# How a two-column offset gets into a constant table: an addition on VectorE, or two index operations on GpSimd

## The chip, the cores and the metric

One core of a Trainium2 chip. The metric is the time of one execution on the device in microseconds (us). The kernel before takes 411.8 us (median of three runs, 411.5 to 411.99). All runs below were judged to be in the fast state. A verdict of "faster" or "slower" needs a change of over 2%, which is 8.2 us here.

## The reference, cut to what matters

The program is an RWKV-style attention (4 batches, 8 heads, 768 tokens, head dimension 48) followed by a mixture of 8 experts in which each token goes to one expert.

```python
for t in range(S):                               # attention, per batch and head
    cur = einsum('bhd,bhe->bhde', u[None] * kt, vt)
    y[:, :, t] = einsum('bhd,bhde->bhe', rt, state + cur)
    state = w[None, :, :, None] * state + einsum('bhd,bhe->bhde', kt, vt)
...
fresh_e = int(np.argmax(logits[b, s]))           # experts: first maximum wins
e = fresh_e if s == 0 or local_gate[b, s] < 0.5 else prev_e
...
out[b, s] = p[e] * (relu(x[b, s] @ w1[e]) @ w2[e])
```

The kernel has to sort the experts by how many tokens each got. `tie` is a constant table of 8 numbers (the same on all 128 partitions) that makes equal counts distinct and moves the first two experts down by a fixed amount. It matters only that `tie` holds the right eight numbers by the time that the experts are sorted, late in the program.

## The kernel before

Attention runs as 16 items (a batch and a pair of heads). TensorE does the matrix products of an item; GpSimd scales keys and receptances for the item to come (`ke`, `rw`, `pd`); VectorE masks scores (`am`), scans states (`S`) and scales keys (`kw`); loads run some three items ahead. The table is made in passing while item 6 is in work:

```python
def constants(self, part):                       # part 2, in the item loop at n = 5
    ...
    self.tie = self.iota("tie", [P, E], [[-1, E]], base=E - 1, cast=True)
    self.ief = self.iota("ief", [1, E], [[1, E]], cast=True)

def cast(self):                                  # in the item loop at n = 6
    for f, i in self.casts:
        self.nc.scalar.copy(f, i)                # integer -> float, on ScalarE
    self.casts = []
    self.nc.vector.tensor_scalar(self.tie[:, :EARLY], self.tie[:, :EARLY],
                                 float(-E * TAIL), None, Alu.add)

def blocks(self):                                # 88 us later: the only reader of tie
    ...
    nc.vector.scalar_tensor_tensor(self.c8, end, float(E), self.tie, Alu.mult, Alu.add)
```

The place in the loop, cut to the calls around it:

```python
            if n + 1 < M:
                self.scale(n + 1)                # GpSimd: ke, rw, pd of the next item
            ...
            self.inside(n - 1)
            self.before(n - 1)
            if n == 6:
                router.cast()                    # ScalarE casts, then the addition
            ...
            self.scores(n, 0)()                  # TensorE L284, then VectorE am (L286)
            keep = self.scores(n, 1)
            ...
            self.own(n)                          # TensorE L265
            keep()                               # VectorE: second am
```

In the trace VectorE does its work one after another in this order. The `am` product of item 6 is issued just behind the addition, and the next TensorE group (L319, the `turn` of an earlier item) writes the bank that this `am` has to have read. So the addition stands in front of TensorE, by way of `am`.

## Time and profile before

| of the profiled execution | value |
|---|---|
| span | 410.2 us |
| TensorE busy | 393.6 us, 96% |
| VectorE, GpSimd, ScalarE busy | 37%, 35%, 18% |
| mean granted TensorE clock | 0.983 |
| first expert product / last TensorE instruction | 125.5 us / 402.7 us |

The lines that carry the argument are in the prediction below. Two views complete them. From the page: the busy share of the DMA engines (tenths) and what they moved in each fortieth of the span (10.3 us), and the queue that fetches instructions.

```profile
DMA  7999956999224783600641181253245145163010
GB/s 259 414 422 414 414 200 233 320 318 394 82 54 167 291 342 110 266 0 30 231 200 33 54 306 59 59 190 157 67 154 197 53 150 197 41 229 131 0 35 34
...
q8 instruction: 29, 0.48, 0.4%
```

In slices 2 to 5 (10 to 51 us) the DMA engines are full and move 414 to 422 GB/s; then, during the stall, they fall to 200. The queue at the bottom will matter later: instructions come over the same DMA engines, 0.48 MB of them.

The second is a table of stretches (busy us of each engine and, in brackets, instructions; then the granted clock, the DMA share and GB/s).

```profile
core 0: us, PE busy (x) PEld busy (x) DVE busy (x) ACT busy (x) POOL busy (x), PEclk, DMA share, GB/s
46.00:50.00 4.00, 3.60 (x91) 2.56 (x87) 2.16 (x3) 1.31 (x6) 4.00 (x6) 1.00 1.04 410
50.00:54.00 4.00, 0.00 (x0) 0.00 (x0) 4.00 (x1) 0.00 (x0) 4.00 (x5) 0.68 0.83 336
54.00:56.00 2.00, 0.79 (x4) 0.79 (x5) 2.00 (x4) 0.00 (x0) 0.27 (x1) 0.50 0.10 39
56.00:58.00 2.00, 2.00 (x26) 1.67 (x26) 1.75 (x3) 0.70 (x2) 0.00 (x0) 0.50 0.44 104
...
62.00:64.00 2.00, 2.00 (x54) 1.20 (x45) 1.02 (x2) 0.80 (x1) 1.69 (x3) 1.00 0.69 264
```

From 50 to 54 us TensorE ran nothing and VectorE one instruction. The clock was already falling there (mean 0.68), stayed at 0.50 and was back at 1.00 from 62 us. The clock record itself has one low stretch of 10.24 us, which began about 51.4 us.

### The profile page before, as it was taken

The page shows a single profiled execution, that of the slowest core. Times are in us where ns is not written, and L with a number is a line of the kernel's source. Part 1 is how long each engine was busy: PE and PEld are TensorE (multiplying, and loading weights), DVE is VectorE, ACT ScalarE, POOL GpSimd, SP SyncE. Part 2 cuts the span into 40 slices and gives each one's busy share as a digit, 9 for nine tenths or more (in the row PEclk, how much of TensorE's full clock was granted, in tenths as well). Part 3 has the DMA queues.
Part 4 walks back from the last instruction along what each step waited for, and adds up shares of the span by engine and source line. Part 5 has one row for each costly group of instructions (what it writes and reads, how often), then busy time and mean ns, then how long its engine had stood idle before and what let it go on. Part 6 is the DMA issues. An engine that isn't in the chain of part 4 may idle for free. (4 is left out here: it accounts for less than half of the span.)

```text
span 410.2 us, 8245 instructions
## 1 busy us (share of the span) xinstructions
PE 393.6 (96%) x3427; PEld 280.5 (68%) x3427; DVE 149.9 (37%) x322; ACT 72.9 (18%) x175; POOL 143.7 (35%) x178
## 2 busy tenths in 40 slices
PE   8999869999999999999999999999999999999992
PEld 7777656877768999545555555566666666679972
DVE  7887667688953642312211111121121111021201
ACT  4122202222223111111111110111011111111110
POOL 8689948686340043011423102301401301202011
PEclk9999959999999999999999999999999999999998
DMA  7999956999224783600641181253245145163010
GB/s 259 414 422 414 414 200 233 320 318 394 82 54 167 291 342 110 266 0 30 231 200 33 54 306 59 59 190 157 67 154 197 53 150 197 41 229 131 0 35 34
DMA packets 17468, 74.90 MB, mean 183 GB/s; under 512 B 2734, under 2 KB 6591, under 8 KB 14864
## 3 DMA queue, kind: packets, MB, share of 16 engines
q1 hardware_dynamic: 10048, 56.89, 36.8%
q0 software_dynamic: 3424, 9.54, 7.2%
q10 hardware_dynamic: 3952, 7.87, 5.1%
q8 instruction: 29, 0.48, 0.4%
q14 instruction: 15, 0.12, 0.1%
HBM read 64.85 MB, written 9.54 MB: 181 GB/s over the span
## 5 line engine op out<-in xcount | busy, mean ns | idle before, releaser
L1045 PE MATMUL h<-exT,w1t 128*128 128x192 f32 (+7 forms) x480 | 138.8, 428 | 0.0
L1057 PE MATMUL y<-hT,w2t 128*128 128x192 f32 (+7 forms) x432 | 131.3, 440 | 0.0
L1045 PEld LDWEIGHTS h<-exT,w1t 128*128 128x128 f32 x480 | 86.3, 190 | 37.4 <-issue 14.8
L1057 PEld LDWEIGHTS y<-hT,w2t 128*128 128x128 f32 x432 | 77.3, 190 | 31.9 <-issue 13.2
L1104 POOL DMA_INDIRECT out_dram<-yo,sid x27 | 26.8, 992 | 183.5 <-DVE yo L1103 159.7
L1049 ACT ACTIVATE hT<-h 128x192 f32<-128x192 f32 (+7 forms) x72 | 31.9, 444 | 199.6 <-PE h L1045 195.2
L1032 DVE COPY exT<-etp 128x384 f32<-128x384 f32 (+7 forms) x29 | 14.3, 495 | 98.4 <-PE etp L1031 98.4
L1103 DVE TENSOR_SCALAR yo<-otp,gate 128x384 f32<-128x384 f32 (+7 forms) x27 | 16.6, 616 | 91.6 <-PE otp L1101 91.6
L1018 POOL DMA_INDIRECT xg<-x_d,gid x29 | 29.8, 1026 | 45.7 <-DVE sm L867 25.8
L286 DVE TENSOR_TENSOR am<-pair,kept 128x768 f32<-128x768 f32 x32 | 30.1, 952 | 15.5 <-PE pair L284 15.4
L218 POOL TENSOR_TENSOR pd<-rk 128x384 f32<-128x384 f32 x32 | 31.8, 1014 | 3.2 <-DMA rk<-in_rk_dram 2.2
L293 PE MATMUL y<-am,kv 128*64 128x128 f32 x384 | 28.6, 287 | 0.8 <-DVE y L269 0.6
L214 POOL TENSOR_TENSOR ke<-kv,endT 128x288 f32<-128x288 f32 x32 | 24.9, 798 | 8.6 <-issue 3.9
L231 POOL TENSOR_TENSOR rw<-rk,tab 128x384 f32<-128x384 f32 x26 | 23.6, 926 | 8.2 <-PE y L306 8.2
L293 PEld LDWEIGHTS y<-am,kv 128*64 128x64 f32 x384 | 24.8, 142 | 1.6 <-DVE y L269 1.2
L284 PE MATMUL pair<-rw,kw 48*64 48x64 f32 (+1 forms) x768 | 23.0, 249 | 0.5 <-issue 0.3
L284 PEld LDWEIGHTS pair<-rw,kw 48*64 48x64 f32 x768 | 19.9, 134 | 1.9 <-issue 1.0
L310 ACT COPY xT<-y 128x768 f32<-128x768 f32 (+1 forms) x16 | 12.5, 780 | 40.6 <-PE y L306 40.6
L319 PE MATMUL pair<-ident,xT 128*128 128x128 f32 x90 | 13.8, 292 | 5.7 <-DVE am L286 5.6
L319 PEld LDWEIGHTS pair<-ident,xT 128*128 128x128 f32 x90 | 10.1, 146 | 13.3 <-DVE am L286 11.2
L269 DVE TENSOR_TENSOR y<-y,vT 128x768 f32<-128x768 f32 x16 | 15.4, 962 | 3.1 <-PE y L265 3.0
L1031 PEld LDWEIGHTS etp<-ident,xg 128*128 128x128 f32 (+7 forms) x87 | 10.2, 140 | 8.3 <-issue 5.9
(215 smaller groups left out, 284.3 us busy)
## 6 DMA issues: line engine op xcount, KB each, us to landing
w1t<-in_w_dram SPq DMA_DIRECT2D x9, 1536.0 KB, 6.5
w2t<-in_w_dram SPq DMA_DIRECT2D x9, 1536.0 KB, 7.7
rk<-in_rk_dram SPq DMA_DIRECT2D x15, 768.0 KB, 9.8
kv<-in_kv_dram SPq DMA_DIRECT2D x16, 584.0 KB, 9.1
vT<-in_vT_dram SPq DMA_DIRECT2D x16, 384.0 KB, 7.4
x_d<-x ACTq DMA_DIRECT2D x4, 1152.0 KB, 9.6
w1t<-in_w_dram ACTq DMA_DIRECT2D x1, 1536.0 KB, 8.0
w2t<-in_w_dram ACTq DMA_DIRECT2D x1, 1536.0 KB, 11.2
```

The lines of the kernel that those rows point to most:

```text
L214: nc.gpsimd.tensor_mul(t["ke"][:, p::2], t["k"][:, p::2], spread(self.endT[:, p, hp], 1, C2))
L218: nc.gpsimd.tensor_mul(t["pd"][:, z], t["rT"][:, z], t["kT"][:, z])
L231: engine.tensor_mul(t["rw"][:, z], t["rT"][:, z], spread(pw, 1, z.stop - z.start))
L284: nc.tensor.matmul(sc[f * DP:(f + 1) * DP, h, i, x:], lhsT=t["kw"][q, c, o * DP:(o + 1) * DP], rhs=t["rw"][q, c, x:], start=True, stop=True)
L286: return lambda: nc.vector.tensor_mul(t["am"][:, g], sc, spread(self.kept[:, g:g + 3], 1, 2))
L293: nc.tensor.matmul(t["y"][p * DP:(p + 1) * DP, h, c2 * P:(c2 + 1) * P], lhsT=t["v"][:, (2 * c + h) * DH:(2 * c + h) * DH + DP], rhs=t["am" ...
L319: nc.tensor.transpose(banks[h][:, c2 * P:(c2 + 1) * P], xT[:, h0 + h, c2 * P:(c2 + 1) * P], self.ident)
L1018: self.nc.gpsimd.indirect_dma_start(out=xg[:n], out_offset=None, in_=self.x_d[:rows], in_offset=bass.IndirectOffsetOnAxis(ap=u["gid"][:n, ...
L1045: nc.tensor.matmul(h[:, :n], lhsT=u["w1"][:, m, kk, :], rhs=u["xT"][:, kk, :], start=(kk == 0), stop=(kk == DK - 1))
L1049: nc.scalar.activation(u[m], h[:, :n], Act.Relu)
L1057: nc.tensor.matmul(u["y"][d][:, :n], lhsT=u["w2"][:, m, d * P:(d + 1) * P], rhs=u[m], start=(m == 0), stop=(m == FK - 1))
L1104: nc.gpsimd.indirect_dma_start(out=self.outs.pop(), out_offset=bass.IndirectOffsetOnAxis(ap=u["sid"][:n, c:c + 1], axis=0), in_=yo[:n], in ...
```

## The change

Its intent: build the two parts of `tie` with their final values, by two index operations with different bases, so that no addition is needed on VectorE.

```diff
-            self.tie = self.iota("tie", [P, E], [[-1, E]], base=E - 1, cast=True)
+            self.tie = self.tl("tie", [P, E])
+            for x, (z, base) in enumerate(((slice(0, EARLY), E - 1 - E * TAIL), (slice(EARLY, E), E - 1 - EARLY))):
+                i = self.iota(f"tie{x}", [P, z.stop - z.start], [[-1, z.stop - z.start]], base=base)
+                self.casts.append((self.tie[:, z], i))
             self.ief = self.iota("ief", [1, E], [[1, E]], cast=True)
...
         for f, i in self.casts:
             self.nc.scalar.copy(f, i)
         self.casts = []
-        self.nc.vector.tensor_scalar(self.tie[:, :EARLY], self.tie[:, :EARLY], float(-E * TAIL), None, Alu.add)
```

## The prediction

> **What bounds the kernel now.** I read the page's busy shares first. TensorE (PE) is busy for 96% of the span, VectorE (DVE) for 37%, GpSimd (POOL) for 35%, so work taken off VectorE is worth nothing unless TensorE waits for it. The 40 slices then show one hole in TensorE: slices 5 and 6 of the clock row, the only low ones before the last.
>
> ```profile
> PE   8999869999999999999999999999999999999992
> DVE  7887667688953642312211111121121111021201
> POOL 8689948686340043011423102301401301202011
> PEclk9999959999999999999999999999999999999998
> ```
>
> Next, the waits of TensorE. One stands out, and it comes once:
>
> ```profile
> PE pair L319 <- DVE am L286: 5.6, 1, 5.6
> PE pair L149 <- POOL ident masks.py:199: 1.6, 1, 1.6
> PE y L293 <- DVE y L269: 0.6, 2, 0.4
> ```
>
> TensorE stood for 5.6 us until VectorE had done an `am` product. To see why VectorE was late I read its instructions in order of time from 42 to 64 us (columns: start us, us taken, engine, line, operation, tiles; in brackets the idle time before it and what ended it):
>
> ```profile
> 46.54 0.65 DVE L255 TENSOR_TENSOR_SCAN S<-step,mp 128x240 f32<-128x240 f32 x1
> 49.03 5.27 DVE L652 TENSOR_SCALAR tie<-tie 128x2 f32<-128x2 f32 x1 [1.84 <-ACT tie L650]
> 54.22 0.94 DVE L286 TENSOR_TENSOR am<-pair,kept 128x768 f32<-128x768 f32 x1
> ```
>
> The addition that the change removes (L652) works on two numbers a partition and takes 5.27 us. Then the same stretch of GpSimd:
>
> ```profile
> 43.66 0.13 POOL L598 IOTA tie_i<- 128x8 int32 x1
> 43.75 0.12 POOL L598 IOTA ief_i<- 1x8 int32 x1
> ...
> 47.00 1.96 POOL L218 TENSOR_TENSOR pd<-rk 128x384 f32<-128x384 f32 x2
> 48.93 1.54 POOL L214 TENSOR_TENSOR ke<-kv,endT 128x288 f32<-128x288 f32 x2
> 50.44 1.93 POOL L231 TENSOR_TENSOR rw<-rk,tab 128x384 f32<-128x384 f32 x2
> 52.34 1.93 POOL L218 TENSOR_TENSOR pd<-rk 128x384 f32<-128x384 f32 x2
> 58.14 1.55 POOL L214 TENSOR_TENSOR ke<-kv,endT 128x288 f32<-128x288 f32 x2 [3.87 <-issue]
> ```
>
> GpSimd runs without a gap from before L652 to 52.34 + 1.93 = 54.27, and L652 ends at 49.03 + 5.27 = 54.30. It ended when GpSimd first fell idle: its 5.27 us are a wait for GpSimd, not work. Last, TensorE in order of time:
>
> ```profile
> 47.47 1.27 PE L284 MATMUL pair<-rw,kw 48*64 48x128 f32 x46
> 48.73 0.88 PE L265 MATMUL y<-pd,w_t 48*64 48x384 f32 x8
> 55.22 1.54 PE L319 MATMUL pair<-ident,xT 128*128 128x128 f32 x6 [5.61 <-DVE am L286]
> ...
> 60.56 1.28 PE L306 MATMUL y<-rw,S 48*48 48x128 f32 x18
> ...
> 61.68 1.28 PE L284 MATMUL pair<-rw,kw 48*64 48x128 f32 x46
> ```
>
> The loop runs 16 items (a batch and a pair of heads). I count an item from one 46-matmul score group (L284) to the next. The starts in that view are 27.71, 34.03, 41.70, 47.47, 61.68, 67.47, 75.41, 81.57. An item without router logits takes 5.77 (41.70 to 47.47) or 5.79 (61.68 to 67.47); the one with the addition takes 14.21.
>
> **What the Trainium skill says.** "SBUF — State Buffer", section "Who interferes with whom": a VectorE copy or tensor_scalar in a two-port mode needs the pair of ports that it shares with GpSimd; whoever issues first holds it for the whole instruction, and the other blocks entirely. The trace agrees and shows worse: five more GpSimd instructions began after 49.03, so VectorE lost not one instruction but the whole queue. "VectorE: DVE Perf Modes", section "Mode 2×_2P — use both read ports for one tensor": that mode is for one source, both ends in SBUF, an even outermost dimension, and works at fp32. L652 is such a one (2 columns, in place). L724, another, took 0.93 us on 24 columns and ended at 98.42, where GpSimd's L218 ended at 98.39; L728, on 2 columns in a GpSimd gap, took 0.17. "TensorE: Matmul & The Clock Gate", Part 1: after an idle window of about 3.4 us the clock falls to half until a busy window has passed. The trace has a granted clock of 0.50 from 55.22 to 61.68 and 1.00 in items before and after. "GPSIMD Engine Reference", section 4.1, gives iota to GpSimd; what it costs I take from the trace.
>
> **The change part by part.** Removed: L652, 5.27 us of VectorE plus its 1.84 us wait for the ScalarE cast of `tie`. Values do not change: columns 0 and 1 start at E-1 less E*TAIL, the other six go on from E-1-EARLY.
>
> Added: one more index operation, 0.13 us by the `tie_i` row, on GpSimd at 43.7 us, where it runs over an item ahead of TensorE. One more ScalarE cast, 0.20 us by its row (it ended at 49.0; ScalarE's next work waited 7.7 us for TensorE). Neither is on the path. An index operation reads no tensor and its ports meet no VectorE instruction that matters, so I count both as zero.
>
> Saved on the path, in two terms:
> 1. The idle time. After the L265 group at 48.73 the L319 group follows in an undisturbed item by 0.81 us (62.95 to 63.76), so it would start at 49.54 instead of 55.22: 5.68 us.
> 2. The slow clock. From the start of L319 to the 46-group of L284 an undisturbed item takes 67.47 - 63.76 = 3.71 us (also 47.47 - 43.76 = 3.71); the disturbed one takes 61.68 - 55.22 = 6.46: 2.75 us.
>
> Sum: 8.43 us, or from the periods 14.21 - 5.78 = 8.43. Everything later hangs on TensorE and should move as a block: 411.8 - 8.4 = 403.4 us, span 410.2 - 8.4 = 401.8.
>
> **The rivals.**
> *The lost time is given back: TensorE meets GpSimd or the DMA at once.* For it: GpSimd is busy all of 28 to 54 us, and the DMA engines moved 409 to 419 GB/s until 52 us at full share; during the stall both caught up. Against it: an item costs GpSimd 1.55 + 1.93 + 1.93 = 5.4 us, less than 5.8. With the addition gone, GpSimd (an estimate from these rows) goes straight on at 54.3 with the item that it began at 58.14 before, and TensorE needs that item only two items later, near 63. Transfers: an item is 768 + 584 + 384 KB = 1.78 MB, at 415 GB/s 4.3 us of a 5.8 us item; adding up issues against GB/s by stretch, about 1.2 MB were outstanding at 46.7 us, so a load lands about 6 us after issue and is needed 12 to 14 after. If this rival won, 2 to 4 us would come back: 406 to 408 us.
> *Another VectorE instruction runs into the same lock.* L699, L703, L728, L760 and L761 are one-source operations of 0.16 to 0.17 us that all fell into GpSimd gaps. Gaps exist because GpSimd waits for TensorE to free `rw` and `pd` (waits of 0.25 to 1.5 us from 62 us on). By my estimate GpSimd is back in that rhythm from the 9th or 10th item, before L699, so the same gaps should meet the same instructions. One miss would cost up to a GpSimd pair of 1.9 us, part of it hidden: 404 to 406 us.
> *Only the busy time counts, and TensorE hides it.* VectorE is 37% busy; on this reading the time stays near 411.8. The 5.6 us wait in TensorE's own list speaks against it.
> *Idle time alone.* If the slow clock had another cause than the idle time, only 5.7 us would go: 406.1 us. The clock was low only right after the gap, so I give it little.
>
> **Range and chances.** The runs of before lie within 0.5 us, so the range comes from the reasoning. The centre is 403.4. Jitter of one item and gaps in TensorE's own instruction supply (one of 0.3 us is seen near 33.8 us) make the upper side longer; below 402.6 there is nothing left to save. I take 402.6 to 405.0. The limit of 2% is at 411.8 x 0.98 = 403.6, only 0.2 us above the centre, so the mechanism does not decide the class, and small losses do: 0.55 for faster by over 2%, 0.44 for within 2%, 0.01 for slower.
>
> **What would show it right or wrong.** Right: no `tie` row on VectorE; TensorE's 5.6 us wait for `am` gone; the period from the 47.5 us score group 5.8 to 6.0 us; granted clock 1.00 from 46 to 64 us; GpSimd without its 3.87 us gap; the expert stage the same length, moved forward by about 8.4 us. Wrong: a new VectorE row of over 1 us on a few columns ending with a GpSimd row (second rival); GpSimd or TensorE waiting for `rk`, `kv` or `vT` (first rival); a low clock in spite of no gap (last rival).

## The result, and the profile after

| | before | after |
|---|---|---|
| median of the same rounds | 411.66 us (411.5 to 411.99) | 404.97 us (404.35 to 405.74) |
| ratio, 95% interval | | 0.9837 [0.9814, 0.9861]: within 2% |
| span of the profiled run | 410.2 us | 404.0 us |
| mean granted clock | 0.983 | 0.997 |
| first expert product | 125.52 us | 119.41 us |

A ratio is the mean time of one kernel's fast runs over that of the other's of the same rounds, so not quite the ratio of the medians. The four runs after are two pairs: 404.35 and 404.36, 405.57 and 405.74. The profile is of the 405.74 us run, the slowest of them; that has to be kept in mind, since one of its gaps is absent from other runs.

The page after, in slices:

```profile
PE   7999999899999999999999999999999999999992
PEclk9999999999999999999999999999999999999998
DMA  7999998988028766201922261272244144162011
GB/s 258 410 409 409 407 378 301 331 294 318 5 62 309 311 230 222 117 19 31 328 90 72 83 264 39 61 270 85 67 178 174 54 181 171 41 255 110 0 36 34
...
q8 instruction: 29, 0.48, 0.5%
```

The hole in TensorE's slices 5 and 6 is gone: the clock row has no low slice before the last, and in slices 6 and 7 the DMA row runs on at 9 and 8 where it had 5 and 6. Compare the GB/s of slices 2 to 5: 410, 409, 409, 407, where before it was 414, 422, 414, 414. Nothing in the change asks for that. It comes back below.

The waits of TensorE (us in total, times, longest), largest first:

```profile
PE pair L149 <- POOL ident masks.py:199: 1.6, 1, 1.6
PE y L293 <- issue: 1.2, 1, 1.2
PE y L293 <- DVE y L269: 0.6, 2, 0.4
```

The 5.6 us wait for `am` is gone, as predicted. New is the second line: 1.2 us in which TensorE waited for nothing that the profile shows.

VectorE and GpSimd in order of time (start, us taken, engine, line, operation):

```profile
46.71 0.65 DVE L255 TENSOR_TENSOR_SCAN S<-step,mp 128x240 f32<-128x240 f32 x1
48.40 0.96 DVE L286 TENSOR_TENSOR am<-pair,kept 128x768 f32<-128x768 f32 x1 [1.04 <-PE pair L284]
49.88 0.97 DVE L269 TENSOR_TENSOR y<-y,vT 128x768 f32<-128x768 f32 x1 [0.53 <-PE y L265]
```

No `tie` row is left between the scan and the mask; `am` takes its 0.96 us. The two index operations are here, in one line of two:

```profile
44.45 0.23 POOL L598 IOTA tie_i<- 128x2 int32 x2
...
51.31 1.96 POOL L231 TENSOR_TENSOR rw<-rk,tab 128x384 f32<-128x384 f32 x2
53.22 1.97 POOL L218 TENSOR_TENSOR pd<-rk 128x384 f32<-128x384 f32 x2
55.14 1.56 POOL L214 TENSOR_TENSOR ke<-kv,endT 128x288 f32<-128x288 f32 x2
```

The two pieces, of 2 and 6 columns (the row names the shape of the first alone), took 0.23 us together, and GpSimd goes straight on at 55.14 us with the item that it began at 58.14 us before. The stretches where the clock had been low:

```profile
50.00:54.00 4.00, 4.00 (x84) 3.45 (x85) 3.13 (x4) 0.70 (x3) 4.00 (x5) 1.00 1.04 412
...
56.00:58.00 2.00, 2.00 (x40) 1.83 (x40) 2.00 (x3) 0.70 (x2) 2.00 (x3) 1.00 0.99 390
```

TensorE is busy all of 50 to 54 us and the clock stays at 1.00. Now the TensorE rows: first the place of the old stall, then the one place that is new.

```profile
48.89 0.88 PE L265 MATMUL y<-pd,w_t 48*64 48x384 f32 x8
49.70 0.87 PE L319 MATMUL pair<-ident,xT 128*128 128x128 f32 x6
...
71.59 0.65 PE L293 MATMUL y<-am,kv 128*64 128x128 f32 x4
73.44 1.47 PE L293 MATMUL y<-am,kv 128*64 128x128 f32 x20 [1.19 <-issue]
```

The L319 group follows the L265 group by 0.81 us, which is the figure that the prediction took. But at 71.59 us a group of 24 `y` products breaks off after four and goes on 1.19 us later without a releaser. There are small ones too, seen in the weight loads around 53 us:

```profile
52.77 0.25 PEld L306 LDWEIGHTS y<-rw,S 48*48 48x48 f32 x4 [0.17 <-issue]
53.23 0.49 PEld L306 LDWEIGHTS y<-rw,S 48*48 48x48 f32 x16 [0.21 <-issue]
```

Weight loads of L306 come here after 0.17 us and again after 0.21 us of nothing. Around 59.4 us there is a third such place (0.36 us).

To see what these cost I measured, in every trace, the period of each item: from the start of its L265 group to the next item's. The columns are the first 15 items, counted from 1: item 7 here is the one with n = 6 in the loop, called item 6 above.

```
before     6.42 6.91 6.58 5.99 8.03 5.77 14.22 5.77 7.93 6.16 6.22 6.34 7.94 6.30 7.48
after      6.41 6.91 6.59 6.15 8.03 5.77  6.05 6.19 7.93 7.66 6.21 6.34 7.93 6.29 7.47
```

Item 7 lost 14.22 - 6.05 = 8.17 us. Item 8 gave back 0.42, item 10 gave back 1.50 and item 4 gave back 0.16. The sum of the row falls by 6.1 us, and so does the time of the first expert product. From there to the last TensorE instruction the two kernels take 277.16 and 277.15 us: the expert stage only moved.

### The profile page after: what moved, and what is told of

The parts are those of the page before. It is cut to its first block, busy times and chain, and to the rows that moved or that the text cites. A ratio compares the mean times of both kernels' runs of the same rounds, so it can differ in the third digit from the quotient of the medians.

```text
span 404.0 us, 8246 instructions
## 1 busy us (share of the span) xinstructions
PE 391.1 (97%) x3427; PEld 277.7 (69%) x3427; DVE 145.2 (36%) x321; ACT 72.9 (18%) x176; POOL 143.3 (35%) x179
## 5 line engine op out<-in xcount | busy, mean ns | idle before, releaser
L293 PEld LDWEIGHTS y<-am,kv 128*64 128x64 f32 x384 | 23.9, 136 | 3.0 <-issue 1.4
L284 PE MATMUL pair<-rw,kw 48*64 48x128 f32 (+1 forms) x768 | 22.5, 249 | 1.2 <-ACT end L165 0.6
L269 DVE TENSOR_TENSOR y<-y,vT 128x768 f32<-128x768 f32 x16 | 15.4, 962 | 3.7 <-PE y L265 3.5
L238 DVE TENSOR_TENSOR kw<-rk,inv 128x768 f32<-128x768 f32 (+1 forms) x19 | 15.5, 818 | 0.1
L1103 PEld LDWEIGHTS otp<-ident,yT 128*128 128x128 f32 (+7 forms) x81 | 10.1, 132 | 7.7 <-issue 5.5
```

Source lines behind the costliest of these rows:

```text
L284: nc.tensor.matmul(sc[f * DP:(f + 1) * DP, h, i, x:], lhsT=t["kw"][q, c, o * DP:(o + 1) * DP], rhs=t["rw"][q, c, x:], start=True, stop=True)
L293: nc.tensor.matmul(t["y"][p * DP:(p + 1) * DP, h, c2 * P:(c2 + 1) * P], lhsT=t["v"][:, (2 * c + h) * DH:(2 * c + h) * DH + DP], rhs=t["am" ...
```

## The experiments

They answer two questions. First, is the 5.27 us a wait for GpSimd, or does it belong to the addition itself? Second, where are the missing 1.1 to 2.4 us of the predicted 8.43?

Chips differ, so each kernel is compared with runs of the kernel before on its own chip. On the chip of the first four runs everything is slower (before: 415.3 us, in two groups near 414.6 and 417), and its traces have an extra wait of about 2.1 us at a ScalarE result in the expert stage and, in some, one of 1.4 us near the end of attention. The trace of two_adds, a kernel with the stall, has both, so they do not concern the change.

### The addition's place: late_add

```diff
 def cast(self):
-        self.nc.vector.tensor_scalar(self.tie[:, :EARLY], self.tie[:, :EARLY], float(-E * TAIL), None, Alu.add)
 def blocks(self):
+        nc.vector.tensor_scalar(self.tie[:, :EARLY], self.tie[:, :EARLY], float(-E * TAIL), None, Alu.add)
         nc.vector.scalar_tensor_tensor(self.c8, end, float(E), self.tie, Alu.mult, Alu.add)
```

The kernel before, with the very same instruction moved to just ahead of its reader.

> The kernel before with its addition on VectorE kept as it is, but issued just before the table is first read, after the attention stage, when GpSimd does no elementwise work. Lock theory (the addition waits for the ports that GpSimd holds): it takes 0.15 to 0.2 us, the 5.6 us wait of TensorE is gone and the time is that of the changed kernel, 404 to 406 us, though VectorE still does the addition and there is no second index operation. Rival (the index operations are what is fast, or the order of VectorE's work matters as such): 409 to 412 us.

Measured: 408.03 us (406.79 to 409.38) against 415.3, ratio 0.9843 [0.9823, 0.9862]. All instructions on `tie` (duration in ns min/median/max, then the start in us):

```profile
L734 DVE TENSOR_SCALAR tie<-tie x1: 163/163/163, 129.7 to 129.7; 128x2 f32<-128x2 f32 x1
L736 DVE SCALAR_TENSOR_TENSOR c<-exc,tie x1: 169/169/169, 129.9 to 129.9; 128x8 f32<-128x8 f32 x1
```

The same addition on the same two columns took 163 ns instead of 5.27 us, and the 5.6 us wait of TensorE is absent. The index operation is as it was before. So no index operation is needed for the gain; the moment of the addition is what cost.

### The addition's source: psum_source

```diff
-        self.nc.vector.tensor_scalar(self.tie[:, :EARLY], self.tie[:, :EARLY], float(-E * TAIL), None, Alu.add)
+        early = self.mp[:, 2 * P + 2 + (NCH - 1) * DH:][:, :EARLY]          # free columns of a PSUM bank
+        self.nc.scalar.copy(early, self.tie[:, :EARLY])
+        self.nc.vector.tensor_scalar(self.tie[:, :EARLY], early, float(-E * TAIL), None, Alu.add)
```

The addition stays at its old moment, with GpSimd as busy as before, but reads its two columns from PSUM.

> The kernel before with the addition in its old place on VectorE, but reading its two columns from PSUM, where ScalarE has copied them (one small ScalarE copy more). Lock theory: a one-source operation that reads PSUM needs no shared port, so it takes 0.15 to 0.3 us although GpSimd is busy without a gap, and the time is 404 to 406 us. Rival (VectorE waits there for ScalarE's casts or for another semaphore, and the 5.27 us are not a lock): the addition still takes about 5 us and the time stays at 411 to 412 us.

Measured: 407.39 us (407.34 to 409.34), ratio 0.9842 [0.9821, 0.9863].

```profile
L653 ACT COPY mp<-tie x1: 163/163/163, 49.0 to 49.0; 128x2 f32<-128x2 f32 x1
L654 DVE TENSOR_SCALAR tie<-mp x1: 159/159/159, 49.1 to 49.1; 128x2 f32<-128x2 f32 x1
```

At 49.1 us, where it had taken 5.27 us, the addition took 159 ns. What changed is where it reads from. This is the sharpest of the experiments: same engine, same moment, same amount of work, same busy GpSimd. Here the addition from SBUF to SBUF waited for GpSimd, and the one from PSUM did not. (It is no longer in place, but that is not the cause: in place it took 163 ns in late_add.) (Item 7 took 6.37 us here: the chain cast, copy, addition made VectorE 0.7 us late for one `am`.)

### Cost of the instruction, or of the moment: two_adds

```diff
-        self.nc.vector.tensor_scalar(self.tie[:, :EARLY], self.tie[:, :EARLY], float(-E * TAIL), None, Alu.add)
+        self.nc.vector.tensor_scalar(self.tie[:, :EARLY], self.tie[:, :EARLY], float(-E * TAIL // 2), None, Alu.add)
+        self.nc.vector.tensor_scalar(self.tie[:, :EARLY], self.tie[:, :EARLY], float(-E * TAIL // 2), None, Alu.add)
```

If 5.27 us were the instruction's own cost, two would cost 10.5.

> The kernel before with the addition split in two halves, one after the other in the same place. Lock theory: the first takes 5 us and ends with GpSimd, the second takes 0.15 to 0.2 us because GpSimd has run dry by then; the time is that of the kernel before plus 0 to 0.4 us, 411.5 to 412.2. Rival (such an operation is slow in itself, about 5 us each): 416 to 418 us.

Measured: 415.66 us against 415.3, ratio 1.0013 [0.9994, 1.0031].

```profile
L652 DVE TENSOR_SCALAR tie<-tie x1: 5985/5985/5985, 48.8 to 48.8; 128x2 f32<-128x2 f32 x1
L653 DVE TENSOR_SCALAR tie<-tie x1: 169/169/169, 54.8 to 54.8; 128x2 f32<-128x2 f32 x1
```

The first took 5.99 us and the second 169 ns. One wait is paid here, not one per instruction: the first ended when GpSimd's queue was empty, and the second fell into the gap. (That is not a rule: in short_queue, below, three instructions in a row paid a wait each.)

### The change once more, on the same chip: after_again

No edit: the changed kernel beside the three above.

> The changed kernel once more, to see how far its own times spread and whether the 1.2 us gap that its first profile shows in TensorE at 72.2 us (in the middle of a group of am products, no releaser named) comes again. Theory A (late instructions: the gap is TensorE waiting for its own next block of instructions, fetched by the same DMA engines as the data): the times fall in two groups about 1.2 us apart, near 404.4 and 405.6 us, and a profile shows the gap at the same matmul or nowhere. Theory B (a wait for data from VectorE, GpSimd or a load): one group of times, and the gap in every profile. Saved against the kernel before: 6.0 to 7.4 us.

Measured: 408.87 us (408.68 to 411.22), ratio 0.9869 [0.9847, 0.9892]. The saving is 6.4 us by the medians and 5.4 by the ratio, where 6.0 to 7.4 were expected. Four of the five runs lie within 0.35 us of each other and one is at 411.22, so the two groups 1.2 us apart of theory A don't show here. The two kernels that keep one index operation did at least as well (0.9843 and 0.9842; the intervals overlap, so the difference is not settled). The gap at 73 us was absent in this profile, those at 34.5, 53.6 and 59.8 us were there.

### The slow clock: before_busy and before_busier

The sum of the prediction has two terms, and the second (2.75 us) supposes that the clock fell because TensorE idled. To take the idleness away and leave the stall, I had TensorE do useless transposes into a free part of a bank while it waits, 36 in one kernel and 50 in the other:

```diff
 # in the item loop, ahead of the L319 group
+            if n == 6:
+                for i in range(36):              # before_busier: 50
+                    self.nc.tensor.transpose(mp[:, :P], self.ident, self.ident)
```

> The kernel before with 36 transposes of the identity put into TensorE's program right where it stands idle (about 5.3 us of work at full clock, into a part of PSUM that nobody reads then). The addition still waits for GpSimd. If the slow clock comes from the idle time, as the prediction's second term has it: the granted clock stays at 1.00 from 50 to 62 us, the idle term of 5.7 us stays and the slow-clock term of 2.75 us goes: 2.0 to 3.0 us below the kernel before. If the slow clock has another cause: within 0.7 us of the kernel before, and the clock still falls to 0.50.

Measured: 410.75 us (409.45 to 412.48) against 411.62, ratio 0.9985 [0.9968, 1.0001]. TensorE and the stretches (columns as above):

```profile
49.93 4.15 PE L470 MATMUL mp<-ident 128*128 128x128 f32 x36
56.00 1.00 PE L319 MATMUL pair<-ident,xT 128*128 128x128 f32 x6 [1.92 <-DVE am L286]
```

```profile
54.00:56.00 2.00, 0.08 (x1) 0.00 (x1) 2.00 (x3) 0.00 (x0) 1.06 (x2) 1.00 0.11 47
56.00:58.00 2.00, 2.00 (x26) 1.70 (x27) 2.00 (x3) 0.70 (x2) 0.00 (x0) 0.65 0.11 19
58.00:60.00 2.00, 2.00 (x25) 2.00 (x23) 1.10 (x2) 0.00 (x0) 1.54 (x2) 0.50 0.80 224
```

The transposes lasted only 4.15 us and left an idle 1.92 us. The clock fell all the same, for 3.41 us instead of 10.24 by the clock record. The time fell by 0.9 us, not by the 2.0 to 3.0 expected. So the trial was too short to settle the term, and it showed that 1.92 us of idleness can be enough. Hence a second one, on another chip:

> The kernel before with 50 transposes in the idle time of TensorE instead of 36. With 36 they ended 1.9 us before VectorE released TensorE, the clock still fell to 0.50 for about 3.2 us and the slow-clock term was 1.4 instead of 2.75 us. At 0.115 us each, 50 last 5.8 us, the whole gap. If the slow clock comes from the idle time, it stays at 1.00 from 50 to 62 us, the wait of TensorE shrinks to under 0.7 us, and the time is 1.8 to 3 us below the kernel before. If transposes do not count or another cause holds, the clock falls again and the gain stays at 1 us or less.

Measured: 409.95 us (409.25 to 409.98) against 411.44, ratio 0.9958 [0.9941, 0.9975].

```profile
49.58 5.68 PE L470 MATMUL mp<-ident 128*128 128x128 f32 x50
55.84 0.87 PE L319 MATMUL pair<-ident,xT 128*128 128x128 f32 x6 [0.58 <-DVE am L286]
...
59.37 1.27 PE L284 MATMUL pair<-rw,kw 48*64 48x128 f32 x46
```

```profile
56.00:58.00 2.00, 2.00 (x40) 1.83 (x41) 2.00 (x3) 0.70 (x2) 0.43 (x1) 1.00 0.25 42
58.00:60.00 2.00, 2.00 (x67) 1.83 (x67) 0.93 (x2) 0.32 (x1) 1.41 (x3) 1.00 0.74 235
```

Now 0.58 us of idleness were left and the clock stayed at 1.00. VectorE was stuck as before (its addition took 5.84 us), so the idle term remains and only the clock term goes. Item 7 took 11.85 us instead of 14.22 (the profile of before, from another chip): 2.37 us less. In the prediction's own measure, from L319 to the group of 46, it is 59.37 - 55.84 = 3.53 us against 6.46 before: 2.93 us less, beside the 2.75 predicted. (The item gained less because this run's addition took 0.57 us longer.) The term stands. The time of the whole kernel fell by 1.5 us by the medians and 1.7 by the ratio, a little under the 1.8 to 3 expected; items 11 and 12 gave back 0.43 and 0.14 us.

### The missing part: which gaps, and how often: after_third and after_fourth

No edit: the changed kernel on two more chips, to see which gaps recur.

> The changed kernel a third time, as the reference for the runs beside it. So far: two profiles of it with 407 to 410 GB/s between 10 and 50 us have gaps of 0.1 to 1.2 us in TensorE that no releaser explains, about 260 TensorE instructions (one or two multiples of it) apart, while the two runs that move the addition elsewhere had 411 to 420 GB/s there and no such gap between 45 and 75 us. Theory A (TensorE waits for its own next block of instructions, which queues behind the data): gaps if the rate is about 408, none or a smaller one if it is about 416. Saved against the kernel before 6.0 to 8.5 us.

> The changed kernel as the reference for the three beside it: 0.983 to 0.988 of the kernel before.

Measured: after_third 404.38 us (403.83 to 405.91) against 411.62, ratio 0.9838 [0.9816, 0.9859]; after_fourth 406.71 us against 411.44, ratio 0.987 [0.9844, 0.9896], with its six runs in two groups: 404.27, 404.78, then 406.54, 406.88, 407.11, 407.22. The profiled run of after_third (403.83 us) has no gap at 73 us. That of after_fourth (406.88 us) has it, in the waits of TensorE:

```profile
PE y L293 <- issue: 1.5, 1, 1.5
```

The periods of items 4, 7, 8 and 10, which are the ones that move most (in after_fourth items 1, 6 and 11 are also 0.15 to 0.25 us longer), in the profiles of before, of the changed kernel and of the two kernels without the stall that keep the addition:

```
item            4     7     8    10
before        5.99 14.22  5.77  6.16     addition, stall
after         6.15  6.05  6.19  7.66     run of 405.74 us
after_again   6.16  6.05  6.19  5.94
after_third   5.88  6.05  6.20  5.94     run of 403.83 us
after_fourth  6.26  6.19  6.20  7.94     run of 406.88 us
late_add      5.77  5.78  5.77  5.94     addition moved
psum_source   5.89  6.37  5.77  5.93     0.7 us wait for am in item 7
```

A small loss of 0.3 and 0.4 us in items 7 and 8 is in every profile of the changed kernel; the large one in item 10 is in two of four, and those are from the slow pair or group of their runs. That the two groups of run times are these gaps present and absent is argued from this, since only profiled runs have a trace.

What sits at these places? I numbered TensorE's instructions in the trace (weight loads, products and those that wait on semaphores) from 0 and looked at the DMA queue that carries instructions. It moves blocks of 16384 bytes. The releaser-less gaps of the changed kernel lie at instruction numbers 1217, 1729, 1985, 2241 and 2753, which differ by 256 or multiples of it, and each ends a little after such a block has landed:

```
trace          block landed   TensorE went on   later by
after              32.70           34.20          1.50
after              51.92           53.23          1.31
after              58.06           59.42          1.36
after              71.98           73.44          1.46
after_fourth       52.60           53.92          1.32
after_fourth       58.62           60.12          1.50
after_fourth       73.00           74.41          1.41
```

The plain reading is that at these places TensorE had run out of instructions: it waited for its own program. before_busier speaks for it: its 100 added instructions move the block ends to other places of the program, and its gap of 0.50 us at 86.72 us lies at number 3265, two times 256 after 2753. But no run made a block late or early by itself, so this is read from numbers and times. Before, the block for number 1985 landed at 51.48 us, in the middle of the stall (49.6 to 55.2 us), and cost nothing; the next landed at 60.12 us for products that TensorE reached nearly 7 us later.

### Does traffic make the blocks late? more_traffic and more_act

The first idea was that other data hold the blocks back. If so, more data queued around these items should widen the gaps. Copies of 0.79 MB from device memory to device memory were added, two on the queue of the loads at n = 8 and 9, or three on ScalarE's queue at n = 6, 7 and 8:

```diff
+MORE = (8, 9)                                   # more_act: (6, 7, 8), on nc.scalar
+            if n in MORE:
+                self.nc.sync.dma_start(out=self.more[MORE.index(n)], in_=self.rk_d[0, 0])
```

> The changed kernel with 0.79 MB more to copy, from DRAM to DRAM, in each of the 9th and 10th items (it is issued by SyncE behind their loads, about 57 and 63 us). Nothing waits for it. Theory A (late instructions): TensorE's instruction blocks wait longer behind data, and gaps of 1 to 3 us with no releaser appear in TensorE between 60 and 80 us, at the same block boundaries as before; the time grows by 1.5 to 5 us. Theory B (the missing 1.7 us has nothing to do with the DMA queues): the data has some 6 us of slack, so no change, within 0.5 us of the changed kernel. Third way (the data itself comes late): the gaps are there, but GpSimd or TensorE names rk, kv or vT as its releaser.

> The changed kernel with three extra copies of 0.79 MB from DRAM to DRAM, issued from ScalarE's queue in the 7th, 8th and 9th items (about 49, 55 and 61 us), a larger and earlier dose than the one before, which added 0.9 us. Theory A: the gaps without releaser at TensorE's block boundaries (near 53, 60, 66 and 73 us) grow to 0.5 to 2 us each, 2 to 5 us in all above the changed kernel. Theory B: no such gaps; if the time grows, then by waits of GpSimd or VectorE for rk, kv or vT.

Measured: more_traffic 405.28 us (404.73 to 405.84), 0.9 us above the changed kernel's 404.38 in the same rounds (the two ranges overlap), less than expected; its gaps, from one weight load to the next, were 0.66, 0.79 and 0.75 us at 53.5, 60.0 and 73.2 us. more_act 404.2 us (404.09 to 404.28), ratio 0.9826 [0.9807, 0.9844], no slower than the changed kernel's 406.71 in the same rounds. It kept two of the small gaps, at 53.6 and 59.8 us (0.66 and 0.52 us from one weight load to the next). There was no gap at 73 us, although 2.4 MB more were moved. So the amount of data in the queues does not alone set how late a block comes. The expectation failed, and with it the simple form of this theory.

### Less data ahead: ahead3 and short_queue

```diff
-AHEAD = 4
+AHEAD = 3                                       # ahead3: one buffer of each load fewer
```
```diff
+        i = n if n < AHEAD else 1 + (n - 1) % (AHEAD - 1)      # short_queue: four loads at the start,
+        j = n if n <= AHEAD else 1 + (n - 1) % AHEAD           # then three buffers in rotation
+        rk, vT, kv = self.rks[i], self.vTs[i], self.kvs[j]
...
-            if n + AHEAD - 1 < M:
-                self.load(n + AHEAD - 1)
+            if n == 0:
+                self.load(AHEAD - 1)
+            elif 1 < n < M - 2:
+                self.load(n + 2)
...
+        if b == 2 and h0 == 2:                                 # the write of x of batch 1, two items later
+            self.write_x(1)
```

> The changed kernel loading two items ahead instead of three, so that about 1.8 MB less is queued in the DMA engines at a time; bytes and instructions are the same. Theory A (late instructions): TensorE's blocks of instructions come sooner, the gaps without releaser between 30 and 75 us vanish and the time is 0.5 to 2 us below that of the changed kernel, provided that data does not come late. Theory B: no gain. Third way: the data comes late instead (GpSimd waits for rk or kv), and the time is 1 to 10 us above.

> The changed kernel with a shorter DMA queue: the first four items are loaded as before, later ones one item later (three buffers in turn instead of four), and the write of the second batch of x goes out two items later, out of the stretch in which the 1.2 us gap was seen. Theory A (TensorE's blocks of instructions come late behind data): no gap without a releaser in TensorE between 30 and 75 us, and 0.5 to 1.5 us below the changed kernel of the same rounds. Theory B (the gaps have another cause): as the changed kernel, within 0.4 us. Third way: data comes late and GpSimd waits for rk or kv: slower.

Measured: ahead3 404.74 us (404.09 to 406.0), the same as the changed kernel. The gaps from 30 to 60 us vanished (items 4, 7 and 8 at 5.77), but TensorE waited again at 71.7 us (0.60 us in its products; item 10 at 7.02) and the start took 0.5 us longer, with GpSimd waiting 6.6 us for `kv` instead of 3.5. The wait at 71.7 us has a releaser and is not one for instructions: VectorE's `y` addition (L269) ended late behind two operations on 12 columns (L667, L668) that took 0.71 and 0.93 us instead of the 0.17 each of the changed kernel, which is the prediction's second rival. A gain in one place, lost in others.

short_queue was slower than the changed kernel: 408.92 us (407.61 to 410.77) against 406.71. GpSimd waited 10.3 us for `kv` in seven places and fell behind. The gaps without a releaser, which were to vanish with less data queued, stayed and grew: 0.33 us at 34.1, 0.52 at 47.8 and 1.24 at 55.1 us. GpSimd's delay brought on what the prediction had listed as its second rival. VectorE in order of time, and the TensorE row behind it:

```profile
96.51 0.74 DVE L770 SCALAR_TENSOR_TENSOR si<-r,ei 128x12 int32<-128x12 f32 x1
97.28 0.79 DVE L771 TENSOR_SCALAR si<-si 128x12 int32<-128x12 int32 x1
97.98 0.91 DVE L772 TENSOR_SCALAR si<-si 128x12 int32<-128x12 int32 x1
```

```profile
101.15 1.54 PE L321 MATMUL pair<-ident,xT 128*128 128x128 f32 x6 [2.89 <-DVE am L288]
```

These three operations on 12 columns take 0.16 to 0.17 us each in the changed kernel, where they fall into a GpSimd gap. Here they took 0.74, 0.79 and 0.91, each ending within 0.05 us of the end of one GpSimd operation, because GpSimd was busy without a gap from 93.7 to 101.1 us; TensorE then stood 2.89 us for the `am` behind them. The same lock, met by other instructions, as soon as the rhythm of GpSimd moved.

### A side effect found late, and not tested

In the built programs every load buffer (`rk`, `kv`, `vT`) lies 32 bytes further along its partition after the change than before, because the second small index tile takes another slot in front of them. Before, these addresses were multiples of 64; after, they lie 32 past one. The traces divide along this line, over four chips:

```
                           GB/s, slices 2 to 5    6144-byte packet   instruction block
aligned   before           414 422 414 414            236 ns         0.92 to 0.97 us
          late_add         415 420 416 411            236 ns         0.92 to 0.98 us
          psum_source      415 420 416 414            236 ns
          two_adds         414 420 417 413            236 ns         0.92 to 0.97 us
          before_busy      414 421 415 416            235 ns
          before_busier    415 422 414 413            236 ns
shifted   after            410 409 409 407            241 ns         1.07 to 1.09 us
          after_again      410 410 407 410            241 ns         1.08 to 1.11 us
          after_third      412 409 408 410            241 ns
          after_fourth     410 411 407 408            240 ns         1.06 to 1.10 us
          more_traffic     410 410 408 408            241 ns
          more_act         411 412 407 407            241 ns
```

The packet times are means from 12 to 45 us; the blocks are those fetched from 30 to 50 us. ahead3 and short_queue are left out: they load in another pattern in this stretch (257 and 264 ns). Packets of the shifted kernels take 2% longer (241/236), without an exception, so the loads finish later and the blocks among them too. The two aligned kernels without a stall, late_add and psum_source, have no releaser-less gap from 45 to 75 us, while every shifted one in this table has. That fits a cause: shifted buffers, slower transfers, late blocks. But no run was made of the change with its buffers put back in line (both index operations into one 8-column tile would do it), so this is a correlation and the cause stays open.

The traces also speak against it in part. Aligned kernels have such gaps elsewhere: 0.26 us at 34.0 us in before, 0.16 in psum_source, 0.50 at 86.7 us in before_busier. psum_source may lack the gap at 53 us only because its TensorE came 0.6 us later, held up by `am`: its fetch began 3.75 us after TensorE had passed the block end before, as in the shifted kernels (3.68 to 3.98), and not after 2.84 us as in late_add. And the large gap at 73 us does not come from a slower transfer. There the blocks took 0.94 and 0.93 us in the two profiles of the changed kernel with the gap, and 0.98 and 1.05 in the two without; what differs is when the fetch began, 5.10 and 5.43 us after the block end before, against 3.05 and 2.64. What holds the start back is not known.

## Why the prediction was right or wrong

The predicted time was 403.4 us, with a range of 402.6 to 405.0; measured were 404.97 us, just inside. The class came out as "within 2%", to which it had given a little less weight (0.44) than to "faster by over 2%" (0.55). It had said that the limit lay 0.2 us from its centre and that small losses would decide, and they did.

That the median fell inside is partly luck: two of its four runs lie above 405.0, and the ratios of after_again (0.9869) and after_fourth (0.987), put on 411.8, would give 406.4. Of its signs, the period of the item came out at 6.05 instead of 5.8 to 6.0, and the expert stage moved by 6.1 us instead of 8.4. One reading was loose: it is TensorE's row that is low in slices 5 and 6, the clock row only in the sixth; no sum rests on it.

**The bound.** Right. TensorE's one large wait was the place; VectorE's other 150 us of work never mattered.

**The 5.27 us as a wait for GpSimd.** Right, and shown three ways (that the thing waited for is a shared port is the skill's account, with which they agree): 163 ns at another moment (late_add), 159 ns at the same moment from PSUM (psum_source), 169 ns for a second one right behind (two_adds).

**Idle term, 5.68 us.** Right: L319 follows L265 by 0.81 us after the change.

**Clock term, 2.75 us.** Right; the direct trial (before_busier) gave 2.93 over the same stretch. No low clock is left after. The rival "idle time alone" (406.1 us) falls with it.

**Added work counted as zero.** Right for the engines: two index operations of 0.23 us together and one more cast, none on the path. What the added tile did to the addresses was not thought of.

**"Everything later hangs on TensorE and should move as a block".** This is the step that failed. Item 7 did give 8.17 of 8.43 us, but the profiled run gave 2.1 us back (0.16 + 0.42 + 1.50) and that of after_third 0.4 (item 8). The prediction had it as a tail ("gaps in TensorE's own instruction supply", one of 0.3 us seen near 33.8 us) and put the centre where nothing is lost. The runs show such gaps in every profile of the changed kernel. The stall had let the fetch of TensorE's program get ahead (the block that landed at 60.12 us came nearly 7 us early), and without it, by the reading above, blocks of instructions are waited for. The term that was mis-sized is the saving itself: 8.43 us as an upper bound was right, as the centre it lacked a loss of 0.7 us (0.27 in item 7 and 0.4 in item 8, in every profile of the changed kernel) and of a further 1.5 to 2 us in about half the runs.

**First rival (TensorE meets GpSimd or the DMA at once).** In its words it did not happen: neither engine waited for `rk`, `kv` or `vT` there more than before. In its kind it did: what was given back came from a transfer, only of instructions and not of data. **Second rival.** Not in its one-source operations, which fell into the same gaps as before. But a two-source comparison (`eq`, L663, 96 columns; 0.47 us before) took 0.97 us in the profiled run and 1.52 in after_third, where it ended 0.1 us after a GpSimd row. That is the sign the prediction had named, of over 1 us; item 9, in which it falls, stayed at 7.93 us. On TensorE's path the rival did happen in ahead3 and short_queue. **"Only busy time counts".** Refuted: 6.7 us of time for 4.7 us of VectorE busy time (149.9 to 145.2) on an engine that is 36% busy.

**Open.** Whether the 32-byte shift is what makes the blocks late; why the gap in item 10 comes in about half the runs; what decides when a block is fetched; why the addition waited for five GpSimd operations before the change and the three of short_queue for one each. No kernel here beats the changed one by ratios whose intervals are clear of each other (those of more_act and after_fourth touch at 0.9844).

## What to carry to other kernels

Look at the duration of small VectorE operations: one on two columns that takes microseconds is waiting, and here its end fell on the end of a GpSimd row. Before rewriting it, move it to a moment when GpSimd is idle or let it read from PSUM; either gained all that the rewrite gained. And when a stall is removed, count on a part being taken by what the stall was hiding, here, by all signs, the fetch of the program itself, and check in the built program that a new tile did not move the others.

## What the Trainium skill lacked or had wrong

- "SBUF — State Buffer", "Who interferes with whom", says that the engine that comes second is blocked for the whole of the other's instruction. It lacks that the wait can outlast it: here five more GpSimd instructions began while one VectorE addition waited, 5.27 us (5.99 in two_adds). It need not: in short_queue three waits (0.74, 0.79, 0.91 us) each ended with one GpSimd instruction. Its rule that an instruction with at most one SBUF input outside the two-port modes does not contend agrees with psum_source (159 ns), and its rule that one with two SBUF inputs does contend agrees with the changed kernel, where a comparison of 96 columns (`eq`, L663) took 0.97 us and ended 0.1 us after a GpSimd row; its neighbour of the same size took 0.26.
- "TensorE: Matmul & The Clock Gate", Part 1, has a free-running window of 3413 ns, and the clock records agree (low stretches of 3.413 and 10.240 us, one and three windows). It asks for about one whole idle window before the clock drops; here 1.92 us without work were enough (before_busy; in before the clock fell at 51.45 us, 1.8 us after the last product), and 0.58 us were not (before_busier).
- "Runtime: NRT & Kernel Launch", "Instruction fetch mechanics", has an engine's program refilled in blocks of 16 KiB, 256 instructions, and the traces agree (blocks of 16384 bytes, gaps 256 instructions or multiples of it apart). It calls the cost of crossing a block end mostly hidden; here gaps of up to 1.2 us (after) and 1.5 us (after_fourth) lie at such ends, TensorE going on 1.3 to 1.6 us after the block has landed. It lacks what makes a fetch start late.
- "DMA: Bandwidth & Descriptors", "How a descriptor splits into AXI transactions", tells of 256-byte alignment. What it lacks is a size for large packets into SBUF: with buffers 32 bytes off a multiple of 64, packets of 6144 bytes took 241 ns instead of 236 and loads ran at 407 to 412 GB/s instead of 411 to 422 (a correlation over the 12 profiles of the table above, not undone in a run).
